# Retention and rational feed-forward on one Trainium2 core: the first eight attention units recast in 64-token halves, the second block's stores and the last step reordered

## The chip, the cores and the metric

The kernel runs on one core of one Trainium2 chip. The metric is the device time of a launch in microseconds (us). Before the change it was 907.56 us, the median of three runs from 906.92 to 907.74.

## What is computed

The reference is a linear attention with a decay per head ("retention"), followed by a feed-forward layer whose activation is a quotient of two polynomials. All of it is in fp32, and the eight batches follow one another in one list of 4608 tokens.

```python
# q, k, v: 8 batches x 8 heads x 576 tokens x 64
Dmat = np.where(rel >= 0, gamma[:, None, None] ** rel, 0.0)      # causal, one gamma a head
x    = np.matmul(scale * np.matmul(q, k.T) * Dmat, v)            # -> 4608 tokens x 512
h    = x @ w_in                                                   # 512 -> 2048
P    = a[0] + a[1]*h + a[2]*h*h + a[3]*h*h*h
Q    = 1.0 + abs(b[0])*abs(h) + abs(b[1])*h*h
out  = (P / (Q + 1e-06)) @ w_out                                  # 2048 -> 512
```

## The kernel before

**Feed-forward.** The 4608 tokens are nine blocks of 512. A *step* is one block with one of 16 slices of 128 hidden features: `gemm1` makes h (twelve 128x512 matmuls: the high part of x and w, the low part of x, the low part of w), ACT and DVE work out the quotient (logarithm and exponential on ACT, then a correction on DVE), the result g is split in a high and a low part, and `gemm2`/`gemm2_lo` add twelve more matmuls into the output's accumulators. So a step is 24 matmuls, and there are 144 steps. The accumulators of a block are two tiles `acc` of two PSUM banks each; `evict` (line 819) copies them out on ACT and stores them. The steps run in the order: block 0 with slices 0 to 7, block 1 with slices 0 to 15, block 0 with slices 8 to 15, then blocks 2 to 8. The first 24 steps keep much of their work in PSUM (`early`) and use four banks for h (two of `ps_h`, two of `ps_w`), so `gemm1` can be four steps ahead of the correction that frees a bank (`better`, written `p<-h,p` in the trace). Later `ps_w` is closed, and its banks serve the attention.

**Weights.** Both matrices arrive as 64-bit words, 32 pieces of 512 KB. Each piece (`weight`, line 260) goes through `begin` and `digit` on ACT, `join` and `sign` on DVE, `high_part` on ACT, and `low_part` on GpSimd (POOL) or DVE. `digit` (line 272) turns 16-bit numbers into 32-bit ones (`t<-bits` in the trace). The tile `t` has one buffer.

**Attention.** 36 units of 128 tokens (4.5 to a batch, 4 to a block) are worked off in order; a state S of 64x64 per head is carried from unit to unit and reset at each batch. Each unit loads 512 KB of q and k (`qk`) and 512 KB of k and v (`kv`), q is scaled on POOL (`qk<-qk`) and v on DVE (`kv<-kv`). The first eight units (`attention`, line 375) work on whole units of 128 tokens: eight score matmuls of 64x128, one DVE multiplication of 128x1024 by the mask (`decay`), eight output matmuls of 128x128, eight of 128x64 for the state, and eight of 64x128 for what earlier units contribute. x is then written in a high part by ACT (`xhi<-ps`) and a low part by DVE (`xlo<-ps`). The other 28 units (`visit`, line 512) work on halves of 64 tokens: all matmuls are 64x64, on four quarters of the array, where one PE *visit* does the scores and state steps of unit n+1 and the outputs of unit n together, 64 matmuls. The trace counts two records for each of these fp32 matmuls.

**The order.** A planner (`Plan.run`, line 119) has a list of tasks, each with an engine, a due time, a cost, and what it waits for; it plays the engines' clocks forward and emits the tasks in the order in which they would start. Tables of numbers (`DUE`, `LATE`, `FIRST`, `UNITS`, `HOLD`, `SLACK`, ...) shift the due times. What it emits is kept in order on each engine: an engine's instruction that waits holds up all that is behind it. `LOADS` gives the order of the first loads on SP, the only queue that issues DMAs. Every instruction is recorded with the line of one helper, 69, so views are read by tile names: `h` for `gemm1`, `acc` for `gemm2`, `ps` for attention, `bits`, `c`, `t`, `w` for the weights, `o` for evicted outputs.

**Block 1's end.** Its four banks are evicted one by one into three buffers `cnv`, which the attention also uses: the third and fourth copies need buffers that the first two stores have to free. The next accumulators (block 0, slice 8) need these banks. Lines 840 to 843:

```python
for j in range(2):
    ck = f"o{t}{j}"
    e = add("ACT", i + 3, 0.48, lambda j=j: emit1(j), [t2], [("cnv", ck)], k)
    add("SP", i + 4, 0.35, lambda j=j: sp.dma_start(rows[:, j, :], o_[j]), [e], [], [("cnv", ck)])
```

## Time and profile before

| | us |
|---|---|
| median of the runs | 907.56 |
| the profiled execution | 910.14 |
| its span, first to last instruction | 908.3 |
| PE busy / DVE busy / ACT busy / POOL busy | 889.3 / 787.3 / 653.7 / 156.3 |
| first `gemm1` matmul | 31.25 |
| last matmul ends | 901.6 |

The span is what the trace shows; 1.84 us of the profiled execution lie around it. A row of the timeline gives start, duration, engine, operation, tiles, and in brackets how long the engine had been idle and what ended that. A row of the windows gives, for a stretch of time, each engine's busy time, the TensorE clock that was granted as a share of full speed (PEclk), the share of DMA time and the GB/s. In the chain of waits each row is a start, a duration and what the end of the kernel hung on at that time.

### The profile page before, as it was taken

How to read it: one execution, taken by the hardware profiler on the slowest of the kernel's cores; microseconds unless marked ns; L12 is line 12 of the kernel's file. 1: busy time of each engine (PE TensorE's matmuls, PEld its weight loads, DVE VectorE, ACT ScalarE, POOL GpSimd, SP SyncE). 2: the span in 40 equal slices, each digit the busy share in tenths (PEclk: the TensorE clock that was granted, in tenths of full speed). 3: DMA queues.
4: the chain of work that ended last, by engine and by line, in shares of the span. 5: the costliest groups of instructions: out<-in, count | busy, mean ns of one | idle time of the engine just before them, and what ended most of it. 6: DMA issues, size and time to landing. Idle time of an engine off the chain costs nothing.

```text
span 908.3 us, 17676 instructions
## 1 busy us (share of the span) xinstructions
PE 889.3 (98%) x7344; PEld 736.5 (81%) x7344; DVE 787.3 (87%) x1216; ACT 653.7 (72%) x1017; POOL 156.3 (17%) x133
## 2 busy tenths in 40 slices
PE   6999999989999999999999999999999999999997
PEld 5877888868888888888888888888888888888885
DVE  4899999988998888889998888888888888977975
ACT  3589999964766677666776677667676686677764
POOL 3465564522200000010000000010000000000000
PEclk9999999999999999999999999999999999999999
DMA  9991000022221112111211121111211021001001
GB/s 340 407 408 70 1 1 1 0 96 94 94 90 31 36 35 92 48 47 48 94 47 48 47 95 48 47 48 63 78 48 46 21 80 43 1 2 46 1 1 47
DMA packets 20705, 65.57 MB, mean 72 GB/s; under 512 B 2448, under 2 KB 2576, under 8 KB 20624
## 3 DMA queue, kind: packets, MB, share of 16 engines
q1 hardware_dynamic: 20624, 64.44, 19.8%
q8 instruction: 57, 0.93, 0.4%
q14 instruction: 24, 0.20, 0.1%
HBM read 55.00 MB, written 9.44 MB: 71 GB/s over the span
## 4 chain that ended last, share of the span: by engine, by line
PE 93%; DMA 3%; DVE 2%; ACT 1%; SPq 0%; issue 0%; POOL 0%; ACTq 0%; DVEq 0%; POOLq 0%
PE acc L69 43%; PE h L69 42%; PE ps L69 8%; DMA bits<-in_w_in 2%; DMA out<-o 1%; DVE p L69 0%; DVE c L69 0%; SPq L69 0%; DVE s L69 0%; ACT o L69 0%; DVE xlo L69 0%; POOL w L69 0%; ACTq L948 0%; DVE w L69 0%; DVE h L69 0%
## 5 line engine op out<-in xcount | busy, mean ns | idle before, releaser
L69 PE MATMUL acc<-w,g 128*128 128x512 f32 x1632 | 394.1, 390 | 2.9 <-ACT o L69 2.9
L69 PEld LDWEIGHTS acc<-w,g 128*128 128x128 f32 x1632 | 306.3, 188 | 67.4 <-ACT o L69 3.3
L69 PE MATMUL h<-xhi,w 128*128 128x512 f32 x1152 | 311.5, 393 | 0.3 <-DVE p L69 0.2
L69 PEld LDWEIGHTS h<-xhi,w 128*128 128x128 f32 x1152 | 213.7, 188 | 46.5 <-DVE p L69 1.1
L69 ACT ACTIVATE p<-h,ab_sb 128x512 f32<-128x512 f32 x143 | 110.9, 775 | 92.3 <-PE h L69 91.8
L69 DVE TENSOR_TENSOR p<-p,h 128x512 f32<-128x512 f32 x144 | 98.5, 684 | 67.9 <-ACT u L69 63.7
L69 PE MATMUL h<-xlo,w 128*128 128x512 f32 x576 | 154.3, 390 | 0.0
L69 DVE SCALAR_TENSOR_TENSOR p<-p,ab_sb,h 128x512 f32<-128x512 f32 x168 | 124.7, 744 | 6.9 <-ACT u L69 3.7
L69 PEld LDWEIGHTS h<-xlo,w 128*128 128x128 f32 x576 | 108.2, 188 | 23.1
L69 ACT ACTIVATE u<-v,qc 128x512 f32<-128x512 f32 x120 | 86.8, 724 | 51.4 <-DVE v L69 51.4
L69 ACT ACTIVATE g<-p 128x512 fp32r<-128x512 f32 x136 | 85.6, 630 | 52.6 <-DVE p L69 50.3
L69 ACT ACTIVATE v<-u,absb 128x512 f32<-128x512 f32 x124 | 101.1, 816 | 3.7
L69 DVE SCALAR_TENSOR_TENSOR p<-p,ab_sb,u 128x512 f32<-128x512 f32 x120 | 95.6, 797 | 4.5 <-ACT u L69 4.5
L69 ACT ACTIVATE u<-h 128x512 f32<-128x512 f32 x144 | 84.7, 588 | 4.4 <-DVE v L69 3.1
L69 DVE SCALAR_TENSOR_TENSOR p<-v,p 128x512 f32<-128x512 f32 x120 | 83.0, 691 | 4.0
L69 DVE TENSOR_TENSOR v<-v,u 128x512 f32<-128x512 f32 x120 | 82.7, 689 | 2.5 <-ACT v L69 2.1
L69 DVE SCALAR_TENSOR_TENSOR v<-v,u 128x512 f32<-128x512 f32 x120 | 83.8, 698 | 0.0
L69 DVE TENSOR_TENSOR g<-p,g 128x512 fp32r<-128x512 f32 x112 | 77.1, 689 | 3.1 <-ACT g L69 2.4
L69 ACT ACTIVATE u<-u 128x512 f32<-128x512 f32 x120 | 74.9, 624 | 2.0
L69 POOL TENSOR_TENSOR qk<-qk,gq_sb 128x512 f32<-128x512 f32 x36 | 49.6, 1379 | 77.8 <-DMA qk<-in_qkv 67.3
L69 PEld LDWEIGHTS ps<-qk 64*64 64x64 f32 (+1 forms) x1024 | 38.5, 147 | 19.4 <-issue 10.5
L69 PE MATMUL ps<-qk 64*64 64x64 f32 (+1 forms) x1024 | 43.9, 236 | 7.5 <-POOL qk L69 6.1
(55 smaller groups left out, 738.7 us busy)
## 6 DMA issues: line engine op xcount, KB each, us to landing
qk<-in_qkv SPq DMA_DIRECT2D x36, 512.0 KB, 4.2
kv<-in_qkv SPq DMA_DIRECT2D x36, 512.0 KB, 5.8
bits<-in_w_in SPq DMA_DIRECT2D x16, 512.0 KB, 10.1
bits<-in_w_out SPq DMA_DIRECT2D x16, 512.0 KB, 10.2
out<-o SPq DMA_DIRECT2D x16, 512.0 KB, 3.3
out<-o SPq DMA_DIRECT2D x4, 256.0 KB, 4.4
gq_sb<-in_gq SPq DMA_DIRECT2D x1, 256.0 KB, 6.8
mask_sb<-in_masks SPq DMA_DIRECT2D x1, 160.0 KB, 6.7
```

Of the source, the lines that this page charges most:

```text
L69: return lambda *a, **k: self.tc.keep_in_program_order(method(*a, **k))
```

## The change

- Units 0 to 7 use the half-unit form too (`early_unit` in place of `attention`): scores, state steps and outputs are the 64x64 matmuls of the later units, the mask is the small one, the decay multiplication is 128x512, and the state takes two DVE additions per unit (`middle`, `grow`). Two accumulator banks of the `acc` ring hold a unit. Where n is in `JOIN = (1,3,4,5,6)`, the outputs of unit n and the scores and state steps of unit n+1 are one PE visit.
- The scaling of q may go to DVE, the fade of the state may go to DVE, and `digit` may go to POOL (`digit_p`). 13 of the 32 digits do.
- The first loads have another order; the 160 KB mask table is gone.
- Block 1's stores are due eight steps sooner, and unit 10's load waits for the copies of block 1's first tile; each later load waits for the one before.
- In the last step, `gemm2` goes through the four banks one after the other with all three products of a bank together, and waits for the low part of g first; the four banks are copied in four ACT instructions and stored in four DMAs of 256 KB.
- The numbers of the tables change (due times, holds, slacks).

```diff
-AHEAD = -6
-FIRST = (-30.37, -29.34, -25.59, -24.33, -24.08, -16.98, -16.13, -17.66)
+JOIN = (1,3,4,5,6)
+AHEAD = -6.09
+FIRST = (-28.56, -27.33, -25.57, -24.53, -22.56, -16.58, -16.78, -16.52)
...
+        def digit_p():
+            c_[1] = cnt.tile([P, DM], I32, tag="t", name=f"t{nm}")
+            pool.tensor_scalar(c_[1], words()[2], 15 * 2.0**-17, None, ALU.mult)
...
-        t = add("ACT", d + DUE["digit"], 0.55, digit, [t], [("t", k)])
+        t = add("ACT", d + DUE["digit"], 0.55, digit, [t], [("t", k)], other=[("POOL", 0.9, digit_p, True)])
...
-        tq = add("POOL", at_(DUE["scale_q"]), 1.21, scale_q, [got[0], consts["gq"]], shared=True)
+        tq = add("POOL", at_(DUE["scale_q"]), 1.21, scale_q, [got[0], consts["gq"]], shared=True,
+                 other=[("DVE", 0.61, scale_q_v, True)])
...
+        def visit_():
+            lanes = no_lanes()
+            begin()
+            scores(n, lanes)
+            steps_of(n, lanes)
+            outputs(n - 1, lanes)
+            pairs(lanes)
...
+        if joined:
+            v = prev["visit"]
+            v.after += [tq, tv]
+            v.takes.append(("acc", key))
+            v.ways["PE"] = (2.0, visit_, False, 0.0)
+            v.due = at_("scores")
+            ts = td = last = v
+        else:
+            ts = add("PE", at_("scores"), 0.9, scores_, [tq], [("acc", key)])
+            td = add("PE", at_("steps"), 0.9, steps_, [ts, tv])
...
+            if last:
+                for t in range(4):
+                    ts = slice(t * P, (t + 1) * P)
+                    acc = accs[b][t // 2][:, t % 2, :]
+                    for j, x in ((0, 0), (1, 0), (0, 1)):
+                        pe.matmul(acc, g[:, x, ts], w[:, j, :], start=False, stop=(x == 1))
...
-                    add("SP", i + 4, 0.35, lambda j=j: sp.dma_start(rows[:, j, :], o_[j]), [e], [], [("cnv", ck)])
+                    add("SP", i - 4, 0.35, lambda j=j: sp.dma_start(rows[:, j, :], o_[j]), [e], [], [("cnv", ck)])
+                    if t == 0:
+                        ahead.append(e)
...
+                for j in range(2):
+                    e = add("ACT", i + 3, 0.5, lambda j=j: emit_last(j), [t2], [ok] if j == 0 else [])
+                    add("SP", i + 4, 0.35, lambda j=j: sp.dma_start(rows[:, j, :], o_[0][:, j, :]), [e])
...
-                got = load_unit(n + 1, d - 3) if n + 1 < NU else None
+                got = load_unit(n + 1, d - 3, ahead if n + 1 == EARLY + 2 else got if n + 1 > EARLY + 2 else ()) if n + 1 < NU else None
```

PE around the first product of the feed-forward, before. `ps2` to `ps5` are attention units 2 to 5, `s` is what DVE's mask multiplication wrote, `S_sb` the carried state, `h0_0` the first step.

```order
L69 MATMUL ps2_282<-s2_304,kv2_138 64x128 x8
L69 MATMUL ps2_282<-kv2_138 64x64 x8
L69 MATMUL ps2_282<-qk2_134,S_sb_105 64x128 x8
L69 MATMUL ps3_309<-s3_339,kv3_145 64x128 x8
L69 MATMUL ps3_309<-kv3_145 64x64 x8
L69 MATMUL ps3_309<-qk3_143,S_sb_105 64x128 x8
L69 MATMUL ps5_404<-qk5_157 128x128 x8
L69 MATMUL h0_0_414<-xhi0_251,w0_0_152 128x512 x4
L69 MATMUL h0_0_414<-xlo0_252,w0_0_152 128x512 x4
L69 MATMUL ps4_432<-qk4_161 128x128 x8
```

And the same place after the change (the two rows that alternate in pairs inside the visit stand once each).

```order
L71 MATMUL ps2_322<-qk2_125,S_sb_101 64x64 x8
L71 MATMUL ps2_322<-qk2_125,S2_sb_102 64x64 x8
L71 MATMUL ps4_503<-qk4_184 64x64
L71 MATMUL ps3_407<-s3_443,kv3_142 64x64 x2
...
L71 MATMUL ps4_503<-kv4_188 64x64
L71 MATMUL ps3_407<-qk3_140,S1_217 64x64 x2
...
L71 MATMUL ps3_407<-qk3_140,S2_sb_102 64x64 x8
L71 MATMUL h0_0_574<-xhi0_251,w0_0_150 128x512 x4
L71 MATMUL h0_0_574<-xlo0_252,w0_0_150 128x512 x4
L71 MATMUL ps5_588<-qk5_173 64x64
```

The outputs of unit 3, which the first product needs, now share a visit with the scores and state steps of unit 4; before, unit 4 came behind the first product.

The loads on SP in the same stretch, after the change, from the first piece of w_out on (`bits1_0`; a piece `bits` is 512 KB, and so is each `qk` and `kv`). The loads ahead of `bits1_0` are the same as before, in another order and without 128 KB of mask.

```order
L71 DMA bits1_0_145<-in_w_out 128x512
L71 DMA bits0_4_148<-in_w_in 128x512
L71 DMA ab_sb_98<-in_ab 128x6
L71 DMA bits0_3_171<-in_w_in 128x512
L71 DMA qk5_173<-in_qkv 128x1024
L71 DMA kv5_175<-in_qkv 128x1024
L71 DMA bits0_6_181<-in_w_in 128x512
L71 DMA qk4_184<-in_qkv 128x1024
L71 DMA kv4_188<-in_qkv 128x1024
L71 DMA qk6_207<-in_qkv 128x1024
L71 DMA kv6_210<-in_qkv 128x1024
```

Unit 4 is behind unit 5 and one weight piece more (`bits0_6`) than before, where `bits0_4` was followed by `bits0_3` and units 5 and 4.

SP at the end of block 1, before: `qk10` and `kv10` are unit 10's loads, `o1_15_0_0` to `o1_15_1_1` the four banks of block 1.

```order
L69 DMA qk10_2034<-in_qkv 128x1024
L69 DMA kv10_2039<-in_qkv 128x1024
L69 DMA out_0<-o1_15_0_0_2051 128x512
L69 DMA out_0<-o1_15_0_1_2054 128x512
L69 DMA out_0<-o1_15_1_0_2090 128x512
L69 DMA out_0<-o1_15_1_1_2093 128x512
```

And after.

```order
L71 DMA out_0<-o1_15_0_0_2287 128x512
L71 DMA out_0<-o1_15_0_1_2290 128x512
L71 DMA qk10_2299<-in_qkv 128x1024
L71 DMA kv10_2306<-in_qkv 128x1024
L71 DMA out_0<-o1_15_1_0_2321 128x512
L71 DMA out_0<-o1_15_1_1_2324 128x512
```

The two stores that free buffers stand ahead of the two loads. On the last step, PE's signal for the copies on ACT comes once for each tile of two banks: of the four copies, the first of each tile waits for it and the second has no wait of its own.

## The prediction

> **What bounds the kernel now.** I read the page first, then the windows, the waits of PE, and the timeline at the places where PE waits.

> ```profile
> span 908.3 us, 17676 instructions
> ...
> PE 889.3 (98%) x7344; PEld 736.5 (81%) x7344; DVE 787.3 (87%) x1216; ACT 653.7 (72%) x1017; POOL 156.3 (17%) x133
> ```

> The profiled execution took 910.14 us, the span and 1.84 around it; the median of the runs is 907.56, 2.58 lower. I make the sum against 910.14 and take it off the median. What a measurement of this kernel can tell from no change is about 0.2%, 1.8 us.

> Next the windows: length, busy time and instructions of PE, PEld, DVE, ACT, POOL, then clock, DMA share and GB/s.

> ```profile
> 0.00:20.00 20.00, 12.46 (x130) 11.40 (x131) 8.55 (x14) 5.64 (x8) 6.15 (x9) 1.00 0.92 332
> 20.00:40.00 20.00, 17.96 (x248) 15.60 (x250) 18.31 (x25) 10.48 (x18) 9.24 (x10) 1.00 1.03 407
> 60.00:182.00 122.00, 121.90 (x536) 99.99 (x535) 119.71 (x185) 120.71 (x208) 69.38 (x52) 1.00 0.10 41
> 300.00:400.00 100.00, 100.00 (x883) 82.90 (x882) 87.04 (x137) 71.52 (x108) 8.31 (x7) 1.00 0.16 54
> ```

> PE is full from 60 us on. Until 182 us DVE and ACT are nearly full too; at 300 us both have room, so there a new order of their instructions costs nothing as long as PE's order stays, and it does. The only places for a gain are the start, the waits of PE, and the end. Of the waits (sum, count, longest) one stands outside the start:

> ```profile
> PE acc L69 <- ACT o L69: 2.9, 1, 2.9
> ```

> **Part 1, the start.** The old form of a unit on PE, unit 2: scores from 22.41, outputs and state from 23.50, the carried part from 25.48 to 26.50.

> ```profile
> 22.41 1.16 PE L69 MATMUL ps<-qk 64*128 64x128 f32 x16 [1.36 <-POOL S_sb L69]
> 23.50 1.47 PE L69 MATMUL ps<-s,kv 128*64 128x128 f32 x15
> ...
> 25.48 1.09 PE L69 MATMUL ps<-qk,S_sb 64*64 64x128 f32 x16
> 26.50 1.47 PE L69 MATMUL ps<-s,kv 128*64 128x128 f32 x15
> ...
> 31.25 1.20 PE L69 MATMUL h<-xhi,w 128*128 128x512 f32 x4
> ...
> 58.82 1.19 PE L69 MATMUL h<-xhi,w 128*128 128x512 f32 x4 [0.17 <-DVE p L69]
> ```

> That is 1.1 + 3.0 = 4.1 us. The new form stands in the later units: 16 scores take 1.0 us (185.09 to 186.08), a whole visit of 64 matmuls 2.02.

> ```profile
> 185.09 1.15 PE L69 MATMUL ps<-qk 64*64 64x64 f32 x32
> 186.08 0.63 PE L69 MATMUL ps<-kv 64*64 64x64 f32 x16
> ...
> 214.29 2.02 PE ps L69 x128
> ```

> Eight units cost about 8 x 4.1 = 33 us before, and about 22 after (five joint visits of 2.0, the rest alone). But only what lies behind the first `gemm1` counts, since until then PE has time to spare. The attention's PE time from the first `gemm1` to the fifth step's (58.82) is this row:

> ```profile
> 31.20:58.80 27.60, 15.31 (x243) 1.00 1.03 407
> ```

> After the change, 8.0 us of attention remain there (three joint visits, 6.0, and unit 7's outputs, 2.0). So 7.3 us go, if the first `gemm1` stays at 31.25. It does not: the order puts unit 4's scores ahead of it. When does unit 4 land? ACT's first touch of a weight piece gives a time to count from.

> ```profile
> 23.88 0.69 ACT L69 ACTIVATE c<-bits 128x512 f32<-128x512 f32 x1 [0.65 <-DMA bits<-in_w_in]
> ```

> This row is `bits0_4`. Up to it the same bytes are queued after the change, less 128 KB of mask (0.3 us at 407 GB/s): 23.5 us. Unit 4's q is five loads of 512 KB further, 1.29 us each at 407 GB/s: 30.0; its v 31.3; unit 6's v, at which DVE stands in line ahead of unit 3's low part, 33.9. With DVE's scaling (0.70 by its row below) and 0.15 for the signal, PE begins the joint visit at 30.85. Its last part needs v, so it ends near 33.2 at full clock. PE has then been idle from about 24.5 to 30.85. What such a gap does, the trace shows at 200.7:

> ```profile
> 200.70:203.10 2.40, 2.38 (x6) 0.62 0.57 219
> 203.10:205.90 2.80, 2.80 (x114) 0.72 0.02 6
> ```

> After 2.92 us without work the granted clock is below full for some 4 us: 2.4 x 0.38 + 2.8 x 0.28 = 1.7 us lost. [...] I take about 1.2 of the 1.7 as lost in the visit: it ends at 34.4. Then ACT's high part (0.6) and the first `gemm1` at 35.1, 3.85 later than before; DVE's low part is ready at 35.75, before the matmuls that need it at 36.0. The fifth `gemm1` would follow after 4 x 2.72 + 8.0 = 18.9 us, at 54.0, but its bank waits for the correction of step 0, which on DVE stands behind unit 7's low part: the outputs of unit 7 end at 53.1, 0.7 for ACT, 0.6 for DVE, 0.7 for the correction, 0.2: 55.3. Before, 58.82: 3.5 us. Bounds: with full clock and no line behind unit 6's v 4.6; with a wait of 0.7 in each of four visits (half of the 1.36 quoted above) 0.7. I take 3.2, since the small gaps of DVE in this stretch fill up first.

> **Is the lead kept until 182 us?** ACT and DVE must come along. By these rows (mean ns a piece) ACT loses 13 digits of 662 ns, 8.6 us; DVE loses seven decays of 1217 and three `w<-c` of 685, and gets seven of 684, seven additions of about 416 and three scalings of 704 more: -10.6 + 9.8, even.

> ```profile
> L69 ACT ACTIVATE t<-bits 128x512 int32<-128x512 uint16 x32 | 21.2, 662 | 1.0 <-DVE c L69 1.0
> L69 DVE TENSOR_TENSOR s<-ps,mask_sb 128x1024 f32<-128x1024 f32 x7 | 8.5, 1217 | 4.1 <-PE ps L69 4.1
> L69 DVE TENSOR_TENSOR kv<-kv,gv_sb 128x512 f32<-128x512 f32 x33 | 23.2, 704 | 2.0 <-DMA kv<-in_qkv 1.8
> L69 POOL TENSOR_TENSOR w<-c,w 128x512 fp32r<-128x512 f32 x28 | 37.0, 1320 | 50.5 <-ACT w L69 50.5
> ```

> POOL's digit is in no row. Its nearest is POOL's 128x512 pass of 1320 ns; with half of that (one input instead of two) and twice it as bounds, 13 digits take 9 to 34 us of the 52.6 that POOL has idle between 60 and 182. So none of the three is late, PE stays full, and the lead is kept. The other cost of POOL work is DVE: a DVE pass that meets one takes 1.12 in place of about 0.7.

> ```profile
> 126.61 1.12 DVE L69 SCALAR_TENSOR_TENSOR c<-bits,c 128x512 int32<-128x512 int32 x1
> ```

> If every digit met one, 13 x 0.43 = 5.6 us; DVE has 2.3 idle in the window, so up to 3.3 of the lead; I take nothing, as such passes are rare.

> **Part 2, block 1's end: -4.4.** The chain of waits:

> ```profile
> 191.53 0.84 ACT o L69 x2
> 192.38 7.06 DMA out<-o
> ...
> 200.07 0.60 ACT o L69
> ...
> 200.72 2.48 PE acc L69 x6
> ```

> The first store needs 7.06 us, as two loads of 512 KB go ahead of it (2 x 1.29 at 407 GB/s). The third copy waits for its buffer until 199.46, and PE for that bank: 2.92 us, and 1.7 for the clock. With the stores ahead, the first takes 7.06 - 2.6 = 4.5 at most (landed at 192.4 + 4.5 = 196.9) and some 2 at the least (an estimate: by the 3.3 of the last store, quoted below, for half as much traffic); I take 195. The third copy (0.60) and its signal would then be through by 196. PE came to that bank at 200.72 - 2.92 = 197.8, so even the late bound leaves it waiting near zero: the stall and the half clock go. Now late could be unit 10, whose load starts some 2 us later; its visit stands 3.6 us further on PE's row than where the stall was, and DVE's scaling of its v stands in front of a g in the queue. Bounds 2.3 (half of both stays) to 2.92 + 1.7 = 4.6; I take 4.4, with 0.2 off for unit 10.

> **Part 3, the last step: -2.0.**

> ```profile
> 898.58 0.69 DVE L69 TENSOR_TENSOR g<-p,g 128x512 fp32r<-128x512 f32 x1 [0.70 <-ACT g L69]
> 901.63 1.94 ACT L69 ACTIVATE o<-acc 128x1024 f32<-128x1024 f32 x2 [3.08 <-PE acc L69]
> 902.68 1.29 SPq L69 DMA_DIRECT2D out<-o x2
> SPq L948 <- DMA out<-o: 3.3, 1, 3.3
> ```

> From PE's end to the span's it is 6.7 us: copies 1.94, then the last store's issue and 3.3 to land. The signal comes once a tile, so the first tile's copies and stores run under the last six matmuls, and 1.1 us of copies (two of 0.5 to 0.6) remain: -0.8. The last store has half the bytes (-0.6) and less ahead of it (up to -0.9): -1.2. The earlier need of the low part of g costs nothing: the third of the last twelve matmuls starts at 899.4, g is there at 899.3. Bounds 0.8 to 2.5.

> **Sum.** 3.2 + 4.4 + 2.0 = 9.6: 910.14 becomes 900.5, and the median 907.56 - 9.6 = 898.0.

> **Rivals.** *The lead is eaten* (20%): the early visits wait for DVE or POOL, or the digits for a free buffer, and PE is full again only where it was. For it: ACT and DVE were full from 60 us on. Against: both have less or equal work. 907.56 - 6.4 = 901.2. *The stall at block 1 stays* (7%), since the stores still share DMA time with unit 10: 907.56 - 5.2 = 902.4. Both together (3%): 905.6, no change that can be told. *All goes as well as the bounds allow* (6%): 4.6 + 4.6 + 2.5 = 11.7: 895.9. *The digits hold up DVE* (4%), the slower side: every digit on POOL blocks a DVE pass for its whole 1.32 us, 17.2 us on an engine with 2.3 to spare: 14.9 lost, 898.0 + 14.9 = 912.9. It decides from 0.92 us blocked per digit, where the gain of 9.6 is gone. Against it: of 185 DVE instructions beside 52 of POOL, the one above is the longest, with 0.43 extra. [...] That the change doesn't do what it says holds in one point, the last step going by tiles and not by banks, and is in the sum.

> **Numbers.** The forecast has 60%: 898.0. The range is 895.8 to 902.5: below, all bounds good; above, the stall that stays. Faster 0.93, same 0.03, slower 0.04.

> **What would show it.** The first `gemm1` near 35.1 with a half clock before it, the fifth near 55.3; PE full from there, and the digits' collisions on DVE few; no wait of PE for ACT's copies, and no clock drop after 182 us; under 5 us from PE's last matmul to the end. It is wrong if PE idles between 60 and 182 us, or if DVE passes over 1 us become common there.

## The result, and the profile after

The changed kernel takes **917.56 us** (median of four runs, 916.6 to 918.8) where the kernel before takes 907.34 beside it (four runs, 906.92 to 907.74). The ratio is 1.0113, with an interval of 1.0096 to 1.0131: the change makes the kernel slower by about 10.3 us, more than five times what this measurement can tell from no change. The prediction was a gain of 9.6.

The page of the changed kernel's profiled execution (918.8 us) shows that the loss isn't work: PE is busy for 3.5 us less than before (885.8 against 889.3), and the span is 8.7 us longer.

```profile
span 917.0 us, 18691 instructions
...
PE 885.8 (97%) x7824; PEld 733.7 (80%) x7824; DVE 792.3 (86%) x1222; ACT 648.3 (71%) x1006; POOL 175.0 (19%) x144
```

So work was saved, and more than that was waited away. The windows say where (length; busy time and instructions of PE, PEld, DVE, ACT, POOL; clock, DMA share, GB/s).

```profile
20.00:40.00 20.00, 10.12 (x294) 9.46 (x290) 13.78 (x21) 6.19 (x12) 7.67 (x7) 0.75 1.02 406
40.00:60.00 20.00, 16.89 (x441) 14.27 (x445) 16.24 (x26) 11.08 (x18) 10.41 (x9) 0.90 1.02 406
60.00:100.00 40.00, 37.30 (x297) 30.22 (x288) 36.31 (x57) 34.88 (x60) 29.04 (x21) 1.00 0.32 123
100.00:182.00 82.00, 82.00 (x363) 67.92 (x362) 80.38 (x121) 76.57 (x128) 60.51 (x43) 1.00 0.00 1
```

Between 20 and 40 us PE worked 10.12 us; before it was 17.96. And its clock was 0.75 there, where it had been full. From 100 to 182 us PE is full, as it was.

Next, the start times of the same step in both traces, which is how a loss is placed in time. The first `gemm1` starts at 44.85 (before 31.25: 13.6 later), the fifth at 69.55 (before 58.82: 10.7 later); steps 26 and 28 (counted from 0) run 11.2 and 11.6 later, and from step 42 on every step runs 8.66 later, to the end. So the whole loss arises before the first `gemm1`, 2.9 of it come back by the fifth, the time from there to block 1's end passes it on with 0.8 more, block 1's end gives 2.9 against that run of the kernel before, and the tail gives nothing. The new order of the first loads isn't the loss: PE's first score matmul starts at 9.74, and before at 10.37.

The chain of waits leads through the start of the execution (start, duration, what the end hung on; "issue" is time without a releaser in the trace).

```profile
21.21 0.61 DVE s L71
21.86 1.17 PE ps L71 x32
23.13 0.43 DVE S_sb L71
23.59 0.43 DVE S_sb L71
24.06 3.37 PE ps L71 x126
27.43 0.59 ACT xhi L71
28.04 0.70 DVE xlo L71
...
30.39 4.40 PE ps L71 x100
34.80 5.82 issue
40.62 3.56 PE ps L71 x112
44.20 0.61 ACT xhi L71
44.85 2.11 PE h L71 x8
```

Two things are to be seen. Up to 34.80 the chain goes back and forth between PE and DVE: scores, mask, outputs, low part, and again. PE's own order has a part in this: before, PE did unit 1's scores (until 14.09) ahead of unit 0's outputs (from 14.59); now it does them behind these (from 18.26), though unit 1's q was scaled by 14.78. No run here changes that order alone. And PE then stands still for 5.85 us. The view of PE's waits (sum, count, longest):

```profile
PE ps L71 <- issue: 9.0, 5, 5.8
PE ps L71 <- DVE qk L71: 4.9, 1, 4.9
```

The view puts the 5.8 down to "issue"; the timeline shows that PE waits for the scaling of unit 4's q: DVE's scaling of q (`qk<-qk,gq_sb`) ends at 40.52, and PE starts at 40.62. (The 4.9 is the wait for unit 0's load, which was there before.) The timeline of DVE and POOL in that gap:

```profile
34.89 0.42 DVE L71 TENSOR_TENSOR S_sb<-S,ps 128x256 f32<-128x256 f32 x1 [0.97 <-PE ps L71]
...
35.45 0.69 DVE L71 TENSOR_TENSOR xlo<-ps,xhi 128x512 fp32r<-128x512 f32 x1
36.01 1.26 POOL L71 TENSOR_TENSOR w<-c,w 128x512 fp32r<-128x512 f32 x1 [4.06 <-ACT w L71]
36.06 0.41 DVE L71 TENSOR_TENSOR S_sb<-S_sb,ps 128x256 f32<-128x256 f32 x1
36.39 1.44 DVE L71 TENSOR_TENSOR kv<-kv,gv_sb 128x512 f32<-128x512 f32 x1
37.24 1.06 POOL L71 TENSOR_TENSOR S_sb<-S_sb,gv_sb 128x256 f32<-128x256 f32 x1
37.75 1.10 DVE L71 SCALAR_TENSOR_TENSOR c<-c,t 128x512 int32<-128x512 int32 x1
38.26 1.71 POOL L71 TENSOR_TENSOR qk<-qk,gq_sb 128x512 f32<-128x512 f32 x1
38.77 1.75 DVE L71 TENSOR_TENSOR qk<-qk,gq_sb 128x512 f32<-128x512 f32 x1
```

Unit 4's q had landed at 30.71 (the forecast was 30.0). But on DVE its scaling is the last of this row of six. The first of them is unit 3's first addition to the state, and it overwrites the half-way state that unit 2's outputs on PE still read until 34.8. The last three each ran beside a POOL instruction and took 1.44, 1.10 and 1.75 us, where the next three DVE passes of that size (at 40.44, 41.04 and 41.64), with POOL idle, took 0.68 each: by these rows an estimated 2.2 us of the wait, which no run here takes away by itself.

Block 1's end went as forecast: the waits of PE from 185 to 230 us are 0.8 in two for `p`, 0.4 and 0.2, none of them for ACT's copies, and the first store, issued at 204.02, landed 2.06 us later.

### The profile page after: what moved, and what is told of

Read it like the earlier page. It is cut to its first block, busy times and chain, and to the rows that moved or that the text cites. A ratio compares the mean times of both kernels' runs of the same rounds, so it can differ in the third digit from the quotient of the medians.

```text
span 917.0 us, 18691 instructions
## 1 busy us (share of the span) xinstructions
PE 885.8 (97%) x7824; PEld 733.7 (80%) x7824; DVE 792.3 (86%) x1222; ACT 648.3 (71%) x1006; POOL 175.0 (19%) x144
## 4 chain that ended last, share of the span: by engine, by line
PE 83%; DVE 10%; ACT 3%; issue 2%; DMA 1%; SPq 0%; ACTq 0%; DVEq 0%
PE h L71 38%; PE acc L71 36%; PE ps L71 9%; DVE p L71 4%; DVE c L71 2%; DVE v L71 1%; DVE h L71 1%; DMA qk<-in_qkv 1%; ACT h L71 1%; DMA kv<-in_qkv 1%; ACT p L71 0%; DVE kv L71 0%; ACT g L71 0%; DVE xlo L71 0%; ACT xhi L71 0%
## 5 line engine op out<-in xcount | busy, mean ns | idle before, releaser
L71 DVE SCALAR_TENSOR_TENSOR p<-p,ab_sb,u 128x512 f32<-128x512 f32 x120 | 90.5, 754 | 3.5 <-ACT u L71 3.5
L71 DVE TENSOR_TENSOR g<-p,g 128x512 fp32r<-128x512 f32 x112 | 80.1, 715 | 1.8 <-ACT g L71 1.1
L71 PEld LDWEIGHTS ps<-qk 64*64 64x64 f32 x1152 | 40.6, 144 | 27.1 <-issue 20.4
L71 POOL TENSOR_TENSOR qk<-qk,gq_sb 128x512 f32<-128x512 f32 x33 | 45.3, 1372 | 86.9 <-DMA qk<-in_qkv 86.9
L71 PE MATMUL ps<-qk 64*64 64x64 f32 x1152 | 46.1, 232 | 14.6 <-issue 7.5
```

The lines of the kernel that those rows point to most:

```text
L71: return lambda *a, **k: self.tc.keep_in_program_order(method(*a, **k))
```

## The experiments

Each kernel ran beside the kernel before, on the same chip; the number that counts is the ratio to it, 1.0113 (1.0096 to 1.0131) for the changed kernel. A difference between two rows of under 2 to 2.5 us lies within their intervals. Start times of one step in two profiles of the same order differ by up to 1.1 us: with the digits on ACT, whose order up to 82 us is the changed kernel's, the first `gemm1` starts at 43.77 and not 44.85. In us of 907.5 the experiments read so:

| kernel | ratio to before (95%) | us against before | against the changed kernel |
|---|---|---|---|
| before + last step | 0.9976 (0.9966 to 0.9986) | -2.2 | |
| before + stores | 0.9981 (0.9969 to 0.9993) | -1.7 | |
| before + both | 0.9977 (0.9966 to 0.9987) | -2.1 | |
| unit 4 not joined with unit 3 | 1.0170 (1.0150 to 1.0190) | +15.4 | +5.2 |
| no digit on POOL, order laid anew | 1.0189 (1.0170 to 1.0208) | +17.2 | +6.9 |
| all q scaled on POOL | 1.0154 (1.0137 to 1.0171) | +14.0 | +3.7 |
| a unit's two banks as two tiles | 1.0077 (1.0063 to 1.0091) | +7.0 | -3.3 |
| idle matmuls in PE's gaps | 1.0161 (1.0143 to 1.0179) | +14.6 | +4.4 |
| unit 4's scalings moved ahead | 1.0090 (1.0075 to 1.0106) | +8.2 | -2.1 |
| two buffers for the half-way state | 1.0121 (1.0105 to 1.0137) | +11.0 | +0.7 |
| digits issued on ACT, same order | 1.0130 (1.0112 to 1.0149) | +11.8 | +1.5 |
| two tiles + moved + two buffers | 1.0077 (1.0060 to 1.0094) | +7.0 | -3.3 |
| later weight loads | 1.0085 (1.0067 to 1.0103) | +7.7 | -2.5 |
| these four together | 1.0038 (1.0025 to 1.0050) | +3.4 | -6.8 |
| these four + idle matmuls | 1.0036 (1.0023 to 1.0050) | +3.3 | -7.0 |

The theory after the result: the early units' new form loses the time in its hand-overs between PE and DVE. The rivals: the order (unit 4 ahead of the first `gemm1`), the digits on POOL, the half clock after PE's gaps, and a loss in the last two parts.

### The last step and the stores, alone and together

The kernel before gets the new last step only (the edit is the part of the change's diff under `if last:`), then the new stores only, then both.

```diff
-add("SP", i + 4, 0.35, lambda j=j: sp.dma_start(rows[:, j, :], o_[j]), [e], [], [("cnv", ck)])
+add("SP", i - 4, 0.35, lambda j=j: sp.dma_start(rows[:, j, :], o_[j]), [e], [], [("cnv", ck)])
+if t == 0:
+    ahead.append(e)
...
```

> The kernel before with the new last step alone (bank by bank, four copies, four stores); every other instruction stands as before. By the prediction's third part 2.0 us less: near 905.3. By what the changed kernel's profile shows of its end (from the last matmul to the end of the span 5.0 us in place of 6.25, but some 0.2 of waiting for the low part of g in this order): 1.0 less, near 906.3. Third theory, that the new last step is worth nothing, since the step ended 19.1 us after the last gemm1's second part in both profiles: 907.3.

> The kernel before with the second block's stores due sooner and unit 10's load behind them, nothing else. By the prediction's second part 4.4 us less, near 902.9, with no wait of PE and no half clock between 182 and 215 us. By the small waits that the changed kernel's profile has there (0.17, 0.38 and 0.64 in place of 2.92 and 1.7 of lost clock): 3.2 less, near 904.1. If the stall only moves to unit 10's visit: no change, 907.3.

> The kernel before with the second block's stores and the new last step, but with the old early units, tables and digits. If the two add up (ratios 0.9981 and 0.9976 alone): 0.9957, 3.9 us less, 903.4 against 907.3. If one takes away the other's room: 905 or more.

Measured: 906.0, 907.21 and 905.97 us, beside 908.4 (twice) and 907.62 for the kernel before. All three are faster, and the sum of the single gains (3.9) is nearly twice the gain of both together (2.1). The single parts were compared with 23 runs of the kernel before that reach up to 912.24. The runs with the new stores lie within 1.6 us (twelve of the one kernel) and 1.2 (eight of the other), those without within 5.0 (these 23) and 2.5 (twelve with the last step alone); beside the kernel with both, twelve runs of the kernel before lie within 2.3. So the stores seem to take away a spread. Where it may come from is seen in the chain of the kernel with the last step only, whose instructions at block 1's end are those of the kernel before:

```profile
193.06 5.56 DMA out<-o
...
198.64 0.61 ACT o L69
...
199.29 1.65 PE acc L69 x6
```

Here the first store took 5.48 us and not 7.06 (the row is the second store's), PE waited 1.43 us (from 197.86) and not 2.92, and its clock stayed full (1.00 from 195 to 215 us). So the profiled run of before, 2.58 us over its median, was one with a long stall, and the forecast took off the median what such a run holds and this one doesn't. From step 29 on this run is 2.94 us ahead of that one with nothing changed there. Its last step then gains 1.16: from the start of the last `gemm1` to the end it is 18.88 us and not 20.04. With the stores as well the profiled run is 3.68 ahead from step 40 on: against a run with the shorter stall the stores give 0.7 (by this pair of profiles) to 1.7 (by their ratio). Neither part is a loss, so the changed kernel's start must lose 11 to 12 us: 10.3 and what the stores give; by the trace it is 11.6 at step 28. All three kernels beat both kernels of this case; the one with both parts (905.97) and the one with the last step alone (906.0) are level.

### Unit 4 behind the first gemm1

```diff
-JOIN = (1,3,4,5,6)
+JOIN = (1,4,5,6)
```

> The changed kernel with JOIN = (1,4,5,6): the outputs of unit 3 are a PE visit of their own ahead of the first gemm1, and unit 4's scores come behind it, as before the change; up to there the order is that of the changed kernel. Theory A, the joint visit is what makes the first gemm1 late (it waits for unit 4's q, which DVE scales at 38.8): the first gemm1 at about 37.5 in place of 44.85, and most of these 7 us are kept: 911 to 913. Rival B, the slow chain of units 0 to 3 and DVE's queue set the pace anyway: the first gemm1 comes sooner but the fifth stays near 69.5, and the time near 917.

Measured: 1.017. The first `gemm1` came earlier, at 39.15 and not 44.85, and still the fifth was 9.6 later than before (10.7 in the changed kernel), and later steps 14. Behind the first `gemm1` the order was laid anew, so the 5.2 us more aren't the price of the joint visit. But an earlier first `gemm1` alone brought nothing: what counts is when the units are through, and what the forecast took for the heart of the matter, unit 4 ahead of the first product, isn't it.

### The digits on POOL, and the scaling of q

```diff
-('POOL', 'digit'): 0.5
+('POOL', 'digit'): 99.0
```

> The changed kernel with all digits on ACT. The first digit that POOL had began at 82 us, after the loss was complete. Theory A, the digits on POOL have no part in the loss: 917.5, within 1.5. Rival B, they hold up DVE (1.52 us each on POOL): 914 or less. Rival C, ACT needs the relief from 80 to 182 us: 920 or more, with PE idle there.

```diff
-('DVE', 'scale_q'): 0.5
+('DVE', 'scale_q'): 99.0
```

> The changed kernel with every scaling of q on POOL, as before the change. Theory A, unit 4's q scaled on DVE (38.8 to 40.5, behind unit 5's v and a weight's step) is what PE waits for 5.85 us: without it the first gemm1 some 3 to 5 us sooner, the time 912 to 914. Rival B, POOL scales slower (1.3 in place of 0.7 us) and DVE waits for PE anyway: 917 or more.

Both came out slower than the changed kernel, by 6.9 and 3.7 us. Neither can be read as the price of what it names: these numbers steer the planner, and it lays the whole start anew. So the next runs keep the order of the changed kernel word for word. With the same order, 13 digits issued on ACT in place of POOL:

```diff
...
-        for _, emit in seq:
-            emit()
+        for t, emit in seq:
+            (t.ways["ACT"][1] if emit.__name__ == "digit_p" else emit)()
```

> The changed kernel with every instruction in its place, but the 13 digits issued by ACT where POOL issued them (in the earlier test without digits on POOL the planner laid the whole order anew). Theory A, they were a relief for ACT that the second block needs: 13 x 0.66 = 8.6 us more on ACT, which was idle for 5.4 of the 82 us from 100 to 182, so 3 or more us later: 920.5 to 923. Rival B, the digits on POOL hold up DVE (six DVE passes of over 1 us from 80 to 182, one before the change): 914 to 916.

Measured: 1.0130, 1.5 us slower than the changed kernel, with intervals that overlap; the spans of the profiled runs differ by 0.8. So the digits on POOL are not the loss, and a gain of about 1 us from them can't be told from none; the 6.9 above were the new order. In the changed kernel POOL's group of digits reads so (busy, mean ns of one, idle before):

```profile
L71 POOL TENSOR_SCALAR t<-bits 128x512 int32<-128x512 uint16 x13 | 20.4, 1571 | 1.1
```

1.57 us for one, against 1.32 forecast, inside its bounds. DVE's passes over 1 us between 80 and 182 us went from one to six, and with all digits on ACT there are ten, so the digits don't make them; the first digit on POOL starts at 82.46 us, when the loss is already there.

### A unit's two PSUM banks as two tiles

In the changed kernel a unit's scores and outputs lie in one bank and its state steps in the other, but both banks are one tile. PE's outputs of a unit thus wait until DVE has read the state steps as well (unit 1's for 0.94 us, until 24.06), and state steps wait for the mask multiplication (unit 1's for 1.71, until 21.86). With two tiles they don't; the order is the same.

```diff
...
-            ps = ps_acc.tile([P, 2, 512], F32, tag="acc", name=f"ps{n}")
-            bank["s", n] = bank["o", n] = ps[:, 0]
-            bank["ds", n] = ps[:, 1]
+            bank["s", n] = bank["o", n] = ps_early.tile([P, 512], F32, tag="so", name=f"ps{n}")
+            bank["ds", n] = ps_early.tile([P, 512], F32, tag="ds", name=f"ds{n}")
...
```

> The changed kernel with the two PSUM banks of an early unit as two tiles in place of one; every engine's instructions stand in the same order. In the changed kernel PE's outputs of units 0 and 1 started 0.05 us after the second addition to the state (16.00 to 16.06, 24.01 to 24.06), which they don't read, and unit 1's state steps 0.05 after the mask multiplication (21.81 to 21.86), which reads the other bank. Theory A, these waits for a neighbour bank lie on the chain that makes the start late: 0.43, 0.65 and 0.46 us less for units 0 and 1, and as much again for the later ones, so the first gemm1 about 2 us sooner and the time 914 to 916. Rival B, DVE's queue sets the pace, and PE only waits elsewhere: 917.5, within 1.

Measured: 1.0077, 3.3 us better than the changed kernel; by its profile 4.2 at the first step, 2.5 at the fifth, 3.1 at the end. Between unit 0's state steps and unit 3's scores its PE waited for 0.40, 0.20 and 2.52 us, where the changed kernel has 0.98, 1.71, 0.94 and 1.62. The big gap is where it was, only sooner (from the chain):

```profile
30.42 5.82 issue
36.24 1.99 PE ps L71 x64
```

So this is one part of the loss, and it is a false wait: nothing in the computation asks for it.

### Unit 4's scalings ahead of unit 3's mask

In the emitted list DVE's scalings of unit 4's q and v are put ahead of the mask multiplication of unit 3; nothing else moves.

```diff
-            emit()
+            seq.append((t, emit))
...
+        for x, y in (("q4", "mask3"), ("v4", "mask3")):
+            i = next(i for i, (t, _) in enumerate(seq) if t is self.mark[x])
+            one = seq.pop(i)
+            j = next(j for j, (t, _) in enumerate(seq) if t is self.mark[y])
...
+            seq.insert(j, one)
+        for _, emit in seq:
+            emit()
```

> The changed kernel with every instruction in its place but two: on DVE the scalings of unit 4's q and v stand ahead of unit 3's mask multiplication, where DVE had 2.4 us of idle time (30.25 to 32.63; q landed at 30.71, v at 31.99), and no more behind unit 3's first addition to the state, which waits for PE until 34.8. Theory A, the late start is a matter of what stands ahead of unit 4's q in DVE's queue: the visit of units 3 and 4 starts near 35.4 in place of 40.62, the first gemm1 4 to 5 us sooner, and the time 912.5 to 914. Rival B, the visit then waits for something else, or the time is lost again by the fifth gemm1: 916 to 917.5.

Measured: 1.0090, 2.1 us better, at the edge of what the two intervals can tell apart. The gap of 5.85 is down to 2.25, but PE then waits 2.88 for ACT's high part where it waited 0.70: in the profile 3.2 are gained at the first step, 2.0 at the fifth and 2.4 at the end, not 5.85. The chain of this run names what was late next:

```profile
38.82 0.67 ACT t L72
...
39.58 0.89 DVE c L72
...
40.49 0.67 ACT t L72
41.16 0.49 ACT xhi L72
...
41.69 3.67 PE h L72 x8
```

On ACT the high part of unit 3 stands behind two digits, and the second of these waits for a join on DVE. One queue was relieved and the next held the work.

### A second buffer for the half-way state

With one buffer for the state between a unit's two halves, DVE's addition for unit 3 waits until PE has read unit 2's. A second buffer removes that wait; same order.

```diff
+    S2b_sb = op.tile([P, NPAIR, D], F32, tag="o0", name="S2b_sb")
+    def S2_of(n):
+        return S2b_sb if n < EARLY and n % 2 == 0 else S2_sb
...
```

> The changed kernel in the same order, but the early units keep the half-way state in two buffers by turns. In the changed kernel the first addition of unit 3 waited for the outputs of unit 2, which read the one buffer, until 34.8, though unit 3's state steps were done near 32.3, and all of DVE's queue waited behind it. Theory A, this wait is a part of the chain: some 2 us less, 915 to 916. Rival B, DVE would only come to the next wait: 917 to 918.

Measured: 1.0121, no gain. The addition starts 0.9 us sooner, but the low part of x behind it on DVE waits for the same PE visit, and PE's gap is 5.85 us as before. The idea that the missing buffer held the chain falls.

### Idle matmuls in the gaps

29 matmuls of 128x512 into a bank that nobody reads, in four of PE's gaps, so that the clock doesn't fall.

```diff
+    FILL = {("steps", 1): 5, ("visit", 2): 3, ("scores", 3): 5, ("visit", 4): 16}
...
+        for _ in range(FILL.get(at, 0)):
+            pe.matmul(unread, w[:, 0, 0:P], w[:, 0, :], start=True, stop=True)
...
```

> The changed kernel with 29 more matmuls of 128x512 on PE (0.23 us each, of a weight piece with itself, into a bank that nobody reads) in four of the gaps before the first gemm1: 5 ahead of unit 1's state steps, 3 ahead of the visit of units 1 and 2, 5 ahead of unit 3's scores, 16 ahead of the visit of units 3 and 4. Theory A, the half clock behind each gap is a part of the loss: while PE had work, 3.76 us at 0.65, 4.39 at 0.64 and 3.54 at 0.55 of the clock cost 1.3, 1.6 and 1.6; without them the first gemm1 4 us sooner and the time 913 to 914. Rival B, PE would only wait longer for DVE: 916 to 918.

Measured: 1.0161, 4.4 us slower than the changed kernel. The mean clock rose from 0.90 to 1.00 between 40 and 60 us, the joint visit of unit 4 took 2.1 us in place of 3.5, and the first `gemm1` came 1.3 us sooner (43.51); but four waits of PE stood in the trace behind it, with no releaser, of 0.84, 0.95, 2.17 and 1.97 us, and the fifth came 3.4 later:

```profile
PE ps L71 <- issue: 7.6, 5, 2.0
...
PE h L71 <- issue: 2.2, 1, 2.2
```

Such waits are in the changed kernel too (0.38 at 30.02, 0.50 at 52.66, 1.28 at 58.23, 1.01 at 64.70, each in the middle of a visit whose data are all there), and none is in the trace of before. They led to the next experiment.

### Later weight loads

The hypothesis: PE is short of instructions. The page has a DMA queue that it calls `instruction`, 61 packets in 1.00 MB, so blocks of 16 KB (57 before).

```profile
q8 instruction: 61, 1.00, 0.4%
```

In the steady stage their transfers start at 81.87, 111.07, 140.00 and 169.02 us, 29 us apart, the time of 128 matmuls of 128x512 (2.72 us for twelve); with the 64x64 matmuls PE has about five times as many records in the same time (261 in the 12 us from 48 to 60, 363 in the 82 us from 100). In the changed kernel's start the blocks came at 44.53, 50.86, 56.93 and 63.29: 6.2 us apart, with the DMA engines full of loads (406 GB/s from 20 to 66 us). (The times in the expectation below are 11.09 us too late, not counted from the span's start.) The waits of 0.50, 1.28 and 1.01 end 2.31, 2.58 and 2.42 us after the last three of these, and the one of 0.38 ends 2.56 after the block of 27.83; behind the block of 44.53 there is none. The experiment frees the DMA engines: the loads of the weight pieces from slice 8 on and of units 8 and 9, not needed for long, wait until unit 7's high part is written (four small writes on ACT into the pieces' buffers hold them back).

```diff
+        if n == 7:
+            for w in range(2):
+                for f in (8, 9):
+                    tiny = wts.tile([P, 4], F32, tag=f"w{w}_{f}", name=f"tiny{w}_{f}")
+                    act.activation(tiny, o_of(n)[:, 0, 0, 0:4], AF.Copy)
...
```

> The changed kernel in the same order, but the loads of the weight pieces 8 to 15 and of units 8 and 9 wait for unit 7's outputs (ACT writes four tiny tiles into the slots of the first of them), so that DMA is free from about 49 us to 68. It is about waits of PE in the middle of a visit that no other engine ends (0.38 at 30.0, 0.50 at 52.7, 1.28 at 58.2, 1.01 at 64.7), which the kernel before has not. Theory A, PE runs out of code there: the new form issues about twice the instructions, and the 16 KB blocks of code (one for 128 matmuls in the steady stage) came 6.2 us apart (55.6, 61.9, 68.0, 74.4) while loads filled the DMA. With DMA free the last three waits go: 2 to 3 us less, 914.5 to 915.5. Rival B, the waits have another cause: they stay, and the time is 917 to 919.

Measured: 1.0085, 2.5 us better than the changed kernel; in the profile 1.7 at the fifth step. The windows from 48 to 60 us, of the changed kernel first:

```profile
48.00:60.00 12.00, 10.21 (x261) 8.30 (x257) 10.36 (x16) 8.57 (x14) 9.26 (x8) 1.00 1.02 405
```

And with the later loads:

```profile
48.00:60.00 12.00, 12.00 (x372) 10.32 (x376) 8.92 (x16) 8.54 (x14) 7.74 (x8) 0.95 0.01 4
```

With the DMA engines free PE doesn't wait in that stretch at all, and none of the three waits is left in the trace. That these waits go when the DMA engines are free (4 GB/s in place of 405) is shown by this edit; that what came too late was instructions is not shown: it is the author's inference, from the blocks' times and from the lack of any other releaser. Free DMA engines don't rule out that PE stands still: in the kernel with all four edits and idle matmuls, below, it is busy for 11.06 of the 12 us from 48 to 60, where they move 5 GB/s.

### The four together

Two tiles, the moved scalings and the second buffer, first without the later loads, then with them, then with 25 idle matmuls as well (the edits are those above, the idle ones ahead of the visits with the scores of units 2 and 4 and of the first `gemm1`).

> The changed kernel with the scalings of unit 4 moved, two buffers of the half-way state, and the banks of an early unit as two tiles. Theory A, the loss at the start is the chain of waits between PE and DVE, and these three are links of it: by their parts (5, 2 and 2.6 us, overlapping) 908 to 911. Rival B, one link hides the others: 912 to 914, the best of the single ones.

> The changed kernel with unit 4's scalings moved, two buffers of the half-way state, an early unit's banks as two tiles, and the late loads. Theory A (PE short of code is a part of the loss of its own): 2 to 3 us below the kernel with the first three alone (914.3): 911 to 912.5. Rival B, those waits hide behind the chain of DVE: 914 or more.

> As the kernel with the four edits, with 8 idle matmuls of 128x512 ahead of the visit of units 1 and 2, 11 ahead of the visit of units 3 and 4 and 6 ahead of the first gemm1. The same idea alone made the changed kernel 4 us slower, with longer waits in the middle of visits (0.84, 0.95, 2.17, 1.97). Theory A, it was slower since it drained PE's code, and the half clock is still a part of the loss: with DMA free it is now faster than without these matmuls by 1 to 3 us. Rival B, PE waits for DVE as long as before, and the clock does not count: equal or slower.

Measured: 1.0077, 1.0038 and 1.0036. The three without the later loads are, by their medians, no better than the two tiles alone; the later loads then give 3.5 us. All four bring back two thirds of the 10.3. The windows of all four:

```profile
20.00:40.00 20.00, 12.34 (x402) 11.70 (x403) 15.20 (x25) 6.81 (x12) 7.63 (x7) 0.83 1.03 405
40.00:60.00 20.00, 19.73 (x479) 16.13 (x477) 17.45 (x29) 14.04 (x28) 12.01 (x9) 1.00 0.31 119
```

And with the idle matmuls:

```profile
20.00:40.00 20.00, 14.95 (x406) 12.46 (x401) 14.24 (x23) 6.83 (x12) 7.87 (x8) 1.00 1.03 406
40.00:60.00 20.00, 19.06 (x476) 15.73 (x475) 17.82 (x29) 13.21 (x22) 12.26 (x10) 1.00 0.31 123
```

The clock is full throughout, and no time is gained: the joint visit of units 3 and 4 takes 2.1 us and not 3.4, but PE waits for DVE ahead of it and for ACT's high part behind it, and the first `gemm1` starts at 39.81 and 39.45. So in this order the half clock costs nothing beside the gaps; in the changed kernel alone a full clock did bring the first `gemm1` 1.3 us forward, little more than two profiles of one order differ. What remains of the loss shows in the waits of PE, of all four:

```profile
PE ps L72 <- DVE xlo L72: 3.8, 2, 1.9
PE ds L72 <- DVE kv L72: 3.1, 2, 2.4
PE h L72 <- ACT xhi L72: 2.1, 1, 2.1
```

These are the hand-overs themselves, low part and v on DVE and the high part behind the digits on ACT; 1.5 more stand without a releaser. An order that shortens these was not tried; whether the new form could win with it is open, as is where exactly the remaining 3.4 us over before (some 5.5 over before with the two good parts) lie.

## Why the prediction was wrong

**Part 1, the start (forecast a gain of 3.2; measured a loss of 11 to 12).** The step that failed is the sentence that only what lies behind the first `gemm1` counts, since PE has time to spare until then, and with it "PE has then been idle from about 24.5 to 30.85". The forecast counted PE's work and the landing of unit 4, and left out the latencies: units 0 to 3 were taken to be through on PE at 24.5, and their chain through DVE ran to 34.8. The new form has one more trip from PE to DVE and back in each unit, and on DVE unit 4's q stood last of the row of six that began at 34.89. So unit 4's q, which landed at 30.71 as forecast (30.0), was scaled at 38.77 and not at 30.0, and the visit began at 40.62 and not at 30.85: 9.8 of the 14 or 15 us between forecast and outcome are there; the rest comes between the first and the fifth `gemm1`, 24.7 us where 20.2 were forecast. The prediction looked at what stands in front of unit 6's v on DVE, and not at what stands in front of unit 4's q.

The term of PE's work itself was right in kind. From the first to the fifth `gemm1` it was to fall by 7.3 us; the attention's rows took 9.12 and not 15.31, 6.2 less. Of these only 2.9 show, since 3.75 us of new waits lie in that stretch: 2.8 without a releaser (0.50, 1.28, 1.01) and 0.96 for the correction. The waits without a releaser were in no row of before and in no rival.

The clock's cost was there (0.54 in the visit after the long gap, 3.5 us of visit where 2.1 are needed), about as forecast; but the run of all four edits with idle matmuls shows that taking it away gains nothing while the waits stand.

**The lead is kept until 182 us.** This held, and with it what was not meant: a loss is kept as well. The 10.7 us of the fifth step are 11.6 at step 28.

**Part 2, block 1's end (forecast 4.4; measured 0.7 to 1.7 off the median).** The mechanism was right: the first store landed in 2.06 us (2 at the least was forecast), no wait for the copies, no drop of the clock (1.00 from 185 to 230 us). Against the profiled run of before the changed kernel gains 2.9 there, and the kernel with stores and last step 3.7. The size was wrong, since it was read from a run with a stall of 2.92 us where the other profiled run has 1.43 and full clock, and was taken off a median 2.58 lower. The difference between the profiled run and the median was on the page; it was not asked which part of the run it sat in.

**Part 3, the last step (forecast 2.0; alone 1.2 by the traces and 1.3 to 3.1 by the ratio, nothing in the changed kernel).** From PE's last matmul to the span's end it is 5.0 us in place of 6.3; the forecast's 6.7 counts from ACT's first copy, at 901.63, and the last matmul ends at 902.05. In the changed kernel PE waits on the way there:

```profile
905.95 6.05 PE L71 MATMUL acc<-w,g 128*128 128x512 f32 x24 [0.68 <-ACT g L71]
...
908.65 0.69 DVE L71 TENSOR_TENSOR g<-p,g 128x512 fp32r<-128x512 f32 x1 [0.70 <-ACT g L71]
909.39 2.17 PEld L71 LDWEIGHTS acc<-w,g 128*128 128x128 f32 x10 [0.40 <-DVE g L71]
910.64 1.09 ACT L71 ACTIVATE o<-acc 128x512 f32<-128x512 f32 x2 [2.03 <-PE acc L71]
...
912.03 1.08 ACT L71 ACTIVATE o<-acc 128x512 f32<-128x512 f32 x2 [0.30 <-PE acc L71]
```

0.68 for step 14's g, since DVE took three passes of step 15 ahead of step 14's quotient, and 0.40 for the low part of the last g: "the earlier need of the low part of g costs nothing" was off by that (and the third of the last twelve matmuls started at 899.62 before the change, not at 899.4). With the changed order of DVE these two took most of the gain, and the kernel before with the new last step has neither; from the start of the last `gemm1` to the end it is 20.0 us before and 20.1 in the changed kernel.

**The rivals.** "The lead is eaten" had the right place, early visits that wait for DVE, and the wrong bound: it held that the start could at worst be where it was, and so had no price above zero. The one rival on the slower side, digits that hold up DVE, was not it: 1.5 us the other way at most. That a digit blocks a DVE pass for the whole of its time no run shows: the five DVE passes of over 1 us that lie beside a digit in the changed kernel between 80 and 182 us took 1.10 to 1.13 us, 0.4 more than the 0.68 of the same pass with POOL idle (at 33.24).

## What to carry to other kernels

A start that is a chain between two engines is priced by its round trips, with the queue of the slower engine written out instruction by instruction, before any engine's busy time is compared: a form with less work and one more trip can be the longer one (here PE was busy for 3.5 us less, and the kernel took 10.3 more). Two banks that different engines use at different times belong in two tiles (3.3 us here). And a stall taken from one profile is first set beside the median: when the profiled run is some us above it (here 2.58), the stall may be just that (2.92 in one profile, 1.43 in another).

## What was not expected of the hardware

```profile
19.95:23.37 3.42, 1.47 (x40) 1.19 (x36) 2.70 (x5) 1.32 (x3) 0.71 (x1) 1.00 1.02 395
23.37:26.78 3.41, 2.72 (x101) 2.72 (x104) 2.22 (x4) 0.00 (x0) 0.93 (x1) 0.50 1.03 411
26.78:30.19 3.41, 1.61 (x64) 1.36 (x58) 2.57 (x5) 1.80 (x4) 0.37 (x1) 1.00 1.02 404
```

In the first, PE has work for 1.47 us, and the clock is half in the second; in the second for 2.72, and the clock is full in the third. In the 3.41 us ahead of the other two falls PE has work for 1.61 and 1.16 us, in those ahead of the other two returns for 3.21 and 3.23. At block 1's end the clock of the kernel before fell at 201.26, behind 3.41 us with 0.54 of work (the stall of 2.92 lies there), and was full again at 204.68, behind 3.4 us full of work; with the stall of 1.43 in its place, in the kernel with the last step alone, it stayed at 1.00 from 195 to 215 us. Whether the length of a gap or the work beside it decides is not shown.
